# A gated linear-attention cell, a Fourier mixing layer and an MLP in one kernel: third weight piece joined after the fourth block's addition, one conversion fewer per piece, a decay load and some products moved

## The chip, the cores and the metric

The kernel runs on one core of one Trainium2 chip. The metric is the device time of one execution in microseconds (us); a comparison takes the median of several executions. The core's engines are TensorE (PE; PEld is its weight load), VectorE (DVE), ScalarE (ACT), GpSimd (POOL) and SyncE (SP), which here only issues DMAs. Each engine works through its own instructions in the order in which they were recorded.

## The reference

Inputs are four batches of 8 heads, 768 tokens and head size 40. A recurrent cell with exponential gates gives x of shape 4 x 768 x 320; then a Fourier mixing layer and an MLP with two weight matrices held as float64 (320 x 1280 and 1280 x 320) follow.

```
m_new = max(f_gate[t] + m, i_gate[t])
f_stab, i_stab = exp(f_gate[t] + m - m_new), exp(i_gate[t] - m_new)
C = f_stab * C + i_stab * outer(v[t], k[t]);  n = f_stab * n + i_stab * k[t]
y[t] = sigmoid(o_gate[t]) * (C @ q[t]) / max(|n . q[t]|, 1)
...
u   = x + real(fft(fft(x, axis=seq), axis=features))
un  = (u - mean(u)) / sqrt(var(u) + 1e-6)
out = u + relu(un @ w_ch1) @ w_ch2
```

## The kernel before

The recurrence is computed in chunks: 128 tokens (batch 0) or two half chunks of 64 (batches 1 to 3), with a state C carried from chunk to chunk. Per chunk, PE makes scores (ps), the products with the state (ph or hb) and the new state's part (pc); ACT makes the weights W by exponentials; GpSimd scales the queries with the decay (qg, L563, from the loaded Gb), scales the values (vw, L569), masks W (L578) and decays the state (L705); DVE adds to the state (L712), weighs (L717) and finishes x (L768 to L772, L759).

The mixing layer folds x (fe), multiplies with DFT tables along the sequence (pz, copied out as Z and Zt) and along the features (pu, L988). Six blocks of 128 tokens, in the order 0, 5, 1, 4, 2, 3, then go through: the addition of pu to x with mean and variance (`mix_add`, L990: L1004, L1011, L1012 in batch 0; L1006 to L1012 later), the centring on ACT (`mix_center`, uc, L1026), the turn by PE (`mix_turn`, L1037, into put or ph), and ACT's copy into uT (L1042). One row of blocks 1 and 4 needs products of its own: in batch 0 the fourth and fifth product of the second feature group go to hb and are copied by DVE (L1001, L1002) ahead of block 4's addition; in later batches ACT copies them (`mix_own`, L1017, L1018).

The MLP of batch 0 takes uT in ten groups (`IN_ORDER`, L1121): two features' blocks of three products each (L1135) and four quarter-array products for the remaining rows (`rest_products`, L1118). Then the outputs follow (L1273). Batch 0's MLP runs beside batch 1's recurrence. Batches 1 to 3 use sums of weights (L1201, L1330).

The weights come as 64-bit words in ten pieces of 128 x 640 (`class Piece`, L439), built into float32 on the chip: `take` splits exponent e (L463) and upper mantissa m (L465), `convert` turns both on ACT (L471, L473), `join` puts sign and exponent together (L480), adds the lower mantissa (L483) and multiplies (L487). Each piece is loaded by SP (L453, 640 KB) into one of two raw buffers, so a load waits for the L483 of the piece two before.

The order is written out by hand: `at(slot, phase, fn, ...)` enters a step in a plan, and `run` records all steps sorted by slot and phase. A slot is about one step of PE work; phases EVAC, FILL, MAIN and FILL_PE (0 to 3, with fractions between) order the steps within it. PSUM banks are taken in the order of a string (`turn`, L92) or by number. DMAs are issued by SP in the recorded order, on eight semaphores in turn: each issue also waits for the DMA eight before it.

The steps around the change, in the plan's words:

```
for part, (s, phase) in enumerate(((24, -0.1), (26, 0.3), (26, 0.32))):   # L1464
    at(s, FILL + phase, pieces[2].join, part)
at(s_feat[p] + 3, FILL_PE + 5.05, mix_feat, b, p, slice(3, 5))            # L1092: own rows, slot 26
at(a, FILL + 0.05 if b < 2 else MAIN + 0.55, mix_own, b)                  # L1101
at(t + 1 if c < 2 or b > 1 else s - 5, FILL, mlstm_load_decay, b, c)      # L825
```

Batch 0's additions stand in slots 24, 25, 26, 27, 28, 29 at FILL. So DVE records: take of piece 2, L480 of piece 2, additions one to three, L483 and L487 of piece 2, take of piece 3, addition four, additions five and six, join of piece 3.

Of the kernel before, what the change touches and what calls it, by code (L numbers as in the profile page):

```python
# [10 lines left out]
FP = mybir.dt.float32  # L11
# [3 lines left out]
AF = mybir.ActivationFunctionType  # L15
OP = mybir.AluOpType
# [5 lines left out]
NP = H // 2  # L22
# [35 lines left out]
def kernel(  # L58
# [15 lines left out]
    nc = tc.nc  # L74
# [26 lines left out]
    ebias = const.tile([L, 1], FP, name="ebias")  # L101
# [25 lines left out]
    def at(slot, phase, fn, *args):  # L127
        plan.setdefault((slot, phase), []).append((fn, args))
# [7 lines left out]
    EVAC, FILL, MAIN, FILL_PE = range(4)  # L136
# [302 lines left out]
    class Piece:  # L439
# [15 lines left out]
        def take(self):  # L455
            if self.float:
                return
            n = self.src.shape[1]
            words = self.raw.bitcast(U32).rearrange("p (m two) -> p m two", two=2)
            self.lo, self.hi = words[:, :, 0], words[:, :, 1]  # L460
            self.e = cp.tile([L, n], U32, name="e", tag="e", bufs=1)
            self.m = cp.tile([L, n], U32, name="m", tag="m", bufs=1)
            nc.vector.tensor_scalar(out=self.e, in0=self.hi, scalar1=20, scalar2=0x7FF, op0=OP.logical_shift_right,  # L463
                                    op1=OP.bitwise_and)
            nc.vector.tensor_scalar(out=self.m, in0=self.hi, scalar1=0xFFFFF, scalar2=None, op0=OP.bitwise_and)  # L465

        def convert(self, part=None):
            if self.float:
                return
            if part != 1:  # L470
                nc.scalar.activation(out=self.e, in_=self.e, func=AF.Relu, scale=2.0**23, bias=ebias)  # L471
            if part != 0:
                nc.scalar.activation(out=self.m.bitcast(FP), in_=self.m, func=AF.Copy, scale=2.0**-20, bias=1.0)  # L473

        def join(self, part=None):
            if self.float:
                return
            m = self.m.bitcast(FP)
            if part in (None, 0):
                nc.vector.scalar_tensor_tensor(out=self.e, in0=self.hi, scalar=0x80000000, in1=self.e,  # L480
                                               op0=OP.bitwise_and, op1=OP.bitwise_or)
            if part in (None, 1):
                nc.vector.scalar_tensor_tensor(out=m, in0=self.lo, scalar=2.0**-52, in1=m, op0=OP.mult, op1=OP.add)  # L483
            at_ = 0
            for d in self.dst if part in (None, 2) else ():
                r = slice(at_, at_ + d.shape[0])
                nc.vector.tensor_tensor(out=d, in0=m[r], in1=self.e.bitcast(FP)[r], op=OP.mult)  # L487
                at_ += d.shape[0]

    w1_pieces = [Piece([w1_sb[:, n]], w_ch1[:, n * 5 * L:(n + 1) * 5 * L]) for n in range(NFF // 2)]  # L490
# [326 lines left out]
    def plan_halves(b, s0, stride=3):  # L817
        at(s0 - 2, FILL + 0.7, halves_start, b)
        for c in range(NT):
            s = s0 + stride * c  # L820
            end = c == NT - 1
            t = 22 + 2 * c if b == 1 and c < 3 else s - 6
            at(t, FILL, mlstm_load, b, c)
            at(t, FILL, mlstm_load_max, b, c)
            at(t + 1 if c < 2 or b > 1 else s - 5, FILL, mlstm_load_decay, b, c)  # L825
            at(s - 2, FILL, mlstm_load_o, b, c)
            at(s - 2, FILL + 0.1, mlstm_scale_q, b, c)
            at(s - 2, FILL + 0.15, halves_alone, b, c)
            at(s - 1, FILL, mlstm_scale_v, b, c)
            early = (b, c) == (1, 0)  # L830
            at(*((27, FILL + 0.22) if early else (s - 1, FILL)), mlstm_exp, b, c, 0)
            at(*((28, FILL + 0.3) if early else (s - 1, FILL + 0.5)), mlstm_exp, b, c, NP)
            at(s, FILL, mlstm_mask, b, c)
            at(s, FILL_PE + 2.05, halves_scores, b, c)
            at(s, FILL_PE + 2.5, halves_to_state, b, c)
            for i in range(2):
                at(s + i, FILL + 0.05, halves_decay, b, c, i)
                at(s + 1 + i, FILL - 0.2, halves_add, b, c, i)
            at(s + 1, FILL, halves_weigh, b, c)
            if end:  # L840
                for fn, phase in ((halves_from_state, 0.22 if b == 1 else 0.1), (halves_between, 0.23 if b == 1 else 0.15),
                                  (halves_from_chunk, 0.3)):
                    at(s + (1 if b == 1 else 4), MAIN + phase, fn, b, c)
            else:
                at(s + 3, FILL_PE, halves_from_state, b, c)
                at(s + 3, FILL_PE + 0.5, halves_between, b, c)
                at(s + 3, FILL_PE + 3, halves_from_chunk, b, c)
            at(s + 3, FILL_PE + 0.6, mlstm_tanh, b, c)
            at(s + 4, FILL + 0.05 if b == 1 else MAIN + 0.4, mlstm_finish, b, c)
# [216 lines left out]
    def plan_mix(b, s0, x_done, s_feat, s_add, s_turn):  # L1066
        for j in range(TG):
            p = TG - 1 - j
# [18 lines left out]
        for p in range(TG):  # L1087
            for i in range(3) if b == 0 and p == TG - 1 else ():
                at(s_feat[p] + i, FILL_PE + 5.1, mix_feat, b, p, slice(i, i + 1))
            if b == 0 and p == TG - 2:  # L1090
                at(s_feat[p], FILL_PE + 4.06, mix_feat, b, p, slice(0, 3))
                at(s_feat[p] + 3, FILL_PE + 5.05, mix_feat, b, p, slice(3, 5))  # L1092
            elif b == 0 and p == 0:
                at(s_feat[p], FILL_PE + 4, mix_feat, b, p, slice(0, 2))
                at(s_feat[p], FILL_PE + 4.04, mix_feat, b, p, slice(2, 3))
            elif b > 0 or p < TG - 1:
                at(s_feat[p], FILL_PE + 4, mix_feat, b, p)
        for c, a, t in zip(ORDER, s_add, s_turn):
            at(a, FILL if b < 2 else MAIN + 0.5, mix_add, b, c)
            if b > 0 and c == TG - 2:  # L1100
                at(a, FILL + 0.05 if b < 2 else MAIN + 0.55, mix_own, b)  # L1101
            at(*(((32, EVAC + 0.1) if c == 3 else (a, FILL + 0.25) if c in (4, 2) else (t, FILL + 0.1)) if b == 0 else
                 (t, FILL + 0.1)), mix_center, b, c)
            at(t, FILL_PE + (5 if b == 0 or c in ORDER[:4] else -0.1), mix_turn, b, c)
            if b > 0:
                at(t, FILL_PE + 6, mix_turn_out, b, c)
            elif t < s_mlp:
                at(t + 1, FILL + 0.2, mix_turn_out, b, c)
            else:
                at(t + 1, EVAC, mix_turn_out, b, c)  # L1110
# [12 lines left out]
    def mlp_in(b, gr, f):  # L1123


        k = mixes[b]
        u = [uT_bufs[gr][:, ch].rearrange("p c t -> p (c t)") for ch in range(3)]

        n = IN_ORDER.index((gr, f // 2))
        ahead = n > 3 and n % 2 == 1  # L1130
        if f % 2 == 0:
            k.pm = k.pm_next if ahead else [bank("pm", [L, TG * L]) for _ in range(2)]
            k.pms[n] = k.pm
        for i, ch in ((1, 1),) if f % 2 else ((0, 0), (0, 1), (1, 0)):
            nc.tensor.matmul(k.pm[i], w1_block(ch, f // 2 * 2 + i), u[2 * ch], start=(ch == 0 and not ahead),  # L1135
                             stop=(ch == 1 and (ahead or n == 2)), skip_group_check=True)

    def mlp_in_rests(b, n, ahead):

# [225 lines left out]
    def plan_mlp(b, s):  # L1365
# [10 lines left out]
        for gr, n in IN_ORDER if b == 0 else ():  # L1376
            for f in (2 * n, 2 * n + 1):
                at(s, MAIN, mlp_in, b, gr, f)
                s += 1
            i = IN_ORDER.index((gr, n))  # L1380
            if i < 4 or i % 2 == 0:
                at(*((s, MAIN + 0.5) if i == 1 else (s - 1, MAIN + (-0.1 if i == 2 else 0.2))), mlp_in_rests, b, i, False)
                if i > 3:
                    at(s - 1, MAIN + 0.25, mlp_in_rests, b, i + 1, True)
            for f in (2 * n, 2 * n + 1):
                at(s + (i == 1), EVAC, mlp_relu, b, gr, f)
# [63 lines left out]
        at(66 if n == 3 else 57, FILL + 0.41, out_weight_sums, n)  # L1450

    when = [((2, 0.7), (4, 0.5), None), ((18.5, 0.7), (20, 0.7), (21, 0.6)), ((21.5, 0.7), (23, 0.15), None)]
    when += [((26, 0.7), None, (29, 0.5)), ((30, 0.7), (34, 0.7), (35, 0.6))]
    when += [((s, 0.7), (s + 1, 0.7), (s + 2, 0.6)) for s in (36, 39, 42, 48, 51)]
    pieces = w1_pieces + w2_pieces
    for n, (w, p) in enumerate(zip(when, pieces)):
# [4 lines left out]
                at(t[0], FILL + t[1], fn)  # L1461
    for part, s in enumerate((7, 10, 13)):
        at(s, FILL - 0.28, pieces[0].join, part)
    for part, (s, phase) in enumerate(((24, -0.1), (26, 0.3), (26, 0.32))):  # L1464
        at(s, FILL + phase, pieces[2].join, part)
    for part in range(2):
        at(27, FILL + (0.23, 0.3)[part], pieces[3].convert, part)

    early = [(3, mlstm_load, 3), (3, mlstm_load_o, 2), (4, mlstm_load, 4), (5, mlstm_load_decay, 3),
             (5, mlstm_load_decay, 4), (7, mlstm_load_o, 3), (7, mlstm_load, 5),  # L1470
# [159 lines left out]
```

## Time and profile before

| | us |
|---|---|
| median of 3 runs | 389.57 (388.89 to 389.93) |
| the profiled execution | 386.95 |
| its span, first to last instruction | 385.2 |
| PE busy, weight load | 373.1, 274.7 |
| DVE, ACT, POOL busy | 282.2, 176.7, 132.1 |
| granted TensorE clock | 0.999 |

The busy time and the load of the DMAs in four stretches (us from the span's start; the first holds the mixing of batch 0, the second batch 0's MLP beside batch 1's recurrence, the third the first outputs and the mixing of batch 1):

| stretch | length | PE | DVE | ACT | POOL | DMA share, GB/s |
|---|---|---|---|---|---|---|
| 45 to 63 | 18.0 | 14.11 | 16.36 | 11.52 | 3.55 | 0.92, 230 |
| 63 to 104 | 41.0 | 40.28 | 37.09 | 27.10 | 29.31 | 0.88, 245 |
| 104 to 146 | 42.0 | 40.34 | 34.14 | 13.43 | 17.36 | 0.45, 127 |
| 146 to 385.2 | 239.2 | 235.90 | 156.41 | 89.64 | 54.85 | 0.20, 59 |

A line of an engine in order of time reads: start, busy us, engine, line, operation, output<-input, shapes, count, and in brackets the idle time ahead of it and what ended that. Adjacent rows of one engine can overlap by some tenths.

### The profile page before, as it was taken

Reading aid. Unit: us, or ns where it says so; the run is one execution under the profiler, and the core shown is the slowest. Engines: PE = TensorE matmul, PEld = TensorE weight load, DVE = VectorE, ACT = ScalarE, POOL = GpSimd, SP = SyncE. Lnnn points to the kernel's source line nnn. Section 1 sums busy time; section 2 is a strip of 40 time slices with the busy share of each in tenths; the row PEclk is TensorE's granted clock in tenths of the full one; section 3 lists DMA queues with packets and bytes.
Section 4 is the critical chain, followed back from the end, with each engine's and each line's share of the span. In section 5 each row is a group of like instructions: output and inputs, shape, how many; then the busy total and the mean of one; then the engine's idle time right before and its main releaser. Section 6 shows DMA issues by size and latency. Waiting matters only on the chain.

```text
span 385.2 us, 11416 instructions
## 1 busy us (share of the span) xinstructions
PE 373.1 (97%) x4602; PEld 274.7 (71%) x4602; DVE 282.2 (73%) x662; ACT 176.7 (46%) x511; POOL 132.1 (34%) x238
## 2 busy tenths in 40 slices
PE   8999987999999989999999999999999999999996
PEld 6887554566567767756578999656588996546996
DVE  8798998799998584778873787877755785246652
ACT  5988766878262114574443144654530133545000
POOL 4665433875685124363421434561300000020000
PEclk9999999999999999999999999999999999999999
DMA  7869499699981333456001824440000011000000
GB/s 197 281 200 325 137 241 256 189 250 259 258 208 39 108 103 97 144 174 183 1 3 40 207 70 136 146 100 3 0 2 34 1 36 36 0 1 2 35 36 34
DMA packets 21761, 44.00 MB, mean 114 GB/s; under 512 B 3508, under 2 KB 9996, under 8 KB 21580
## 3 DMA queue, kind: packets, MB, share of 16 engines
q1 hardware_dynamic: 21708, 43.27, 39.3%
q8 instruction: 36, 0.59, 0.6%
q14 instruction: 17, 0.14, 0.1%
HBM read 39.16 MB, written 4.10 MB: 112 GB/s over the span
## 4 chain that ended last, share of the span: by engine, by line
PE 79%; DVE 13%; issue 1%; ACT 1%; POOL 0%; DVEq 0%; ACTq 0%; POOLq 0%
PE po L1330 22%; PE pm L1201 19%; PE pm L1118 7%; PE po L1273 7%; PE ph L582 5%; PE ps L582 4%; PE pm L1135 4%; PE pu L988 2%; PE pz L942 2%; PE put L1037 2%; DVE so L772 1%; PE hb L582 1%; PE pzt L942 1%; DVE stats L1011 1%; DVE x L759 1%
## 5 line engine op out<-in xcount | busy, mean ns | idle before, releaser
L1279 DVE SCALAR_TENSOR_TENSOR x<-po,rstd,x 128x160 f32<-128x160 f32 (+1 forms) x69 | 27.1, 393 | 38.4 <-PE po L1330 34.0
L1207 DVE TENSOR_TENSOR h<-h,pm 128x384 f32<-128x384 f32 x60 | 30.5, 549 | 24.7 <-PE pm L1118 11.4
L578 POOL TENSOR_SCALAR_AFFINE_SELECT W<-W 64x512 f32<-64x512 f32 x36 | 28.6, 796 | 38.8 <-ACT W L551 37.6
L1201 PE MATMUL pm<-uT,w_sb 128*128 128x384 f32 x90 | 37.5, 506 | 0.1
L551 ACT ACTIVATE W<-W,colT 128x64 f32<-128x64 f32 x144 | 36.6, 336 | 0.0
L705 POOL TENSOR_TENSOR C<-C,decB 128x164 f32<-128x164 f32 x33 | 18.3, 555 | 52.8 <-DVE C L712 48.6
L1273 PE MATMUL po<-w_sb,h 128*128 128x320 f32 x120 | 33.9, 433 | 0.0
L1118 PE MATMUL pm<-uT,w_sb 64*64 64x384 f32 x320 | 33.2, 497 | 0.0
L563 POOL TENSOR_TENSOR qg<-qk,Gb 128x512 f32<-128x512 f32 x21 | 27.0, 1285 | 12.1 <-DMA qk<-in_qkT 11.1
L1061 POOL TENSOR_TENSOR t<-rstd 128x6 f32<-128x6 f32 x12 | 3.5, 292 | 76.1 <-DVE v L1055 75.6
L1273 PEld LDWEIGHTS po<-w_sb,h 128*128 128x128 f32 x120 | 22.4, 190 | 9.1 <-issue 0.3
L1135 PE MATMUL pm<-uT,w_sb 128*128 128x384 f32 x80 | 28.5, 496 | 0.0
L1330 PE MATMUL po<-T,S 128*128 128x160 f32 x180 | 27.8, 301 | 0.2 <-DVE x L1279 0.2
L1330 PEld LDWEIGHTS po<-T,S 128*128 128x128 f32 x180 | 25.4, 190 | 1.3 <-DVE x L1279 0.4
L1330 PE MATMUL po<-w_sb,h 128*128 128x160 f32 x180 | 26.3, 300 | 0.0
L1330 PEld LDWEIGHTS po<-w_sb,h 128*128 128x128 f32 x180 | 25.2, 190 | 1.4 <-DVE x L1279 0.3
L1201 PEld LDWEIGHTS pm<-uT,w_sb 128*128 128x128 f32 x90 | 15.5, 189 | 12.8 <-DVE h L1207 5.3
L1256 ACT ACTIVATE h<-h 128x384 f32<-128x384 f32 x45 | 23.1, 519 | 2.9 <-DVE h L1207 2.9
L1118 PEld LDWEIGHTS pm<-uT,w_sb 64*64 64x64 f32 x320 | 11.0, 132 | 17.3 <-issue 14.3
L569 POOL TENSOR_TENSOR vw<-kvt,colT 128x328 f32<-128x328 f32 x23 | 19.5, 847 | 4.9 <-DVE shift L211 2.6
L1135 PEld LDWEIGHTS pm<-uT,w_sb 128*128 128x128 f32 x80 | 14.3, 190 | 9.6 <-issue 1.2
L582 PE MATMUL ps<-qk 40*64 40x64 f32 (+1 forms) x768 | 19.1, 235 | 0.0
(255 smaller groups left out, 826.1 us busy)
## 6 DMA issues: line engine op xcount, KB each, us to landing
kvt<-in_kv SPq DMA_DIRECT2D x24, 336.0 KB
qk<-in_qkT SPq DMA_DIRECT2D x48, 160.0 KB
raw<-in_w SPq DMA_DIRECT2D x10, 640.0 KB
Gb<-G_d SPq DMA_DIRECT2D x42, 128.0 KB
W<-M_d SPq DMA_DIRECT2D x36, 128.0 KB
so<-in_o SPq DMA_DIRECT2D x24, 160.0 KB
out<-x SPq DMA_DIRECT2D x23, 160.0 KB
ds_sb<-in_dft_s SPq DMA_DIRECT2D x1, 1158.0 KB
```

Of the source, the lines that this page charges most:

```text
L551: nc.scalar.activation(out=k.W[:, h, :], in_=M, func=AF.Exp, scale=-1.0, bias=colT[:, c, 0, b * H + h:b * H + h + 1])
L563: nc.gpsimd.tensor_tensor(out=k.qg[:, :, t], in0=k.qk[:, 0, :, t], in1=k.Gb[:, :, t], op=OP.mult)
L578: nc.gpsimd.affine_select(out=W, in_=W, compare_op=OP.is_ge, fill=0.0, base=base, pattern=[[0, H], [-1 if back else 1, LH]], channel_multi ...
L582: nc.tensor.matmul(out, w, x, start=start, stop=True, skip_group_check=True)
L1118: nc.tensor.matmul(banks[i][half(cols)], w1_rest(n)[half(i), half(cols)], u[half(i)], start=start, stop=not start, skip_group_check=True)
L1135: nc.tensor.matmul(k.pm[i], w1_block(ch, f // 2 * 2 + i), u[2 * ch], start=(ch == 0 and not ahead), stop=(ch == 1 and (ahead or n == 2)), ...
L1201: nc.tensor.matmul(bank, w, u, start=start, stop=True, skip_group_check=True)
L1207: nc.vector.tensor_tensor(out=h, in0=h, in1=bank, op=OP.add)
L1256: nc.scalar.activation(out=h, in_=h, func=AF.Relu, scale=-1.0)
L1273: nc.tensor.matmul(k.po[m], hidden(gr, f)[:, i * L:(i + 1) * L], w2_sb[:, f, :], start=(f == 0), stop=(f == NFF - 1))
L1279: nc.vector.scalar_tensor_tensor(out=u, in0=po, scalar=k.rstd[:, c:c + 1], in1=u, op0=OP.mult, op1=OP.add)
L1330: nc.tensor.matmul(po, a[:, f], w[:, f], start=start and f == 0, stop=f == half - 1, skip_group_check=True)
```

## The change

It does the following. (1) The third weight piece's join (pieces[2]) is recorded as a whole after the fourth block's addition (27, FILL + 0.13 to 0.15) and ahead of piece 3's take (27, FILL + 0.16); piece 3's conversion is one step. (2) The mantissa is no longer converted by ACT: `take` sets the bit above it as well, L483 adds the lower word scaled by 2^-32 to the integer, and the last multiplication brings a factor 2^-20, as a scalar_tensor_tensor in place of a tensor_tensor. (3) Batch 0's own-row products move ahead of the first turns (slot 24). (4) The decay load of batch 1's first chunk is issued in the slot of its other loads, ahead of a weight load. (5) In batch 1, block 0's centring is recorded ahead of the own-row copies; in batch 0 the centring of blocks 4 and 2 and the exponentials of batch 1's first chunk are re-ordered on ACT. (6) The quarter-array products of batch 0's groups 8 and 9 are no longer made ahead as a pair: group 8's come before its full products, group 9's in its own slot; batch 1's last chunk reads its state two slots later.

```
-            nc.vector.tensor_scalar(out=self.m, in0=self.hi, scalar1=0xFFFFF, scalar2=None, op0=OP.bitwise_and)
-        def convert(self, part=None):
+            nc.vector.tensor_scalar(out=self.m, in0=self.hi, scalar1=0xFFFFF, scalar2=0x100000, op0=OP.bitwise_and,
+                                    op1=OP.bitwise_or)
+        def convert(self):
             if self.float:
                 return
-            if part != 1:
-                nc.scalar.activation(out=self.e, in_=self.e, func=AF.Relu, scale=2.0**23, bias=ebias)
-            if part != 0:
-                nc.scalar.activation(out=self.m.bitcast(FP), in_=self.m, func=AF.Copy, scale=2.0**-20, bias=1.0)
+            nc.scalar.activation(out=self.e, in_=self.e, func=AF.Relu, scale=2.0**23, bias=ebias)
...
-                nc.vector.scalar_tensor_tensor(out=m, in0=self.lo, scalar=2.0**-52, in1=m, op0=OP.mult, op1=OP.add)
+                nc.vector.scalar_tensor_tensor(out=m, in0=self.lo, scalar=2.0**-32, in1=self.m, op0=OP.mult, op1=OP.add)
...
-                nc.vector.tensor_tensor(out=d, in0=m[r], in1=self.e.bitcast(FP)[r], op=OP.mult)
+                nc.vector.scalar_tensor_tensor(out=d, in0=m[r], scalar=2.0**-20, in1=self.e.bitcast(FP)[r], op0=OP.mult,
+                                               op1=OP.mult)
...
-            at(t + 1 if c < 2 or b > 1 else s - 5, FILL, mlstm_load_decay, b, c)
+            at(*((t, FILL + 0.02) if (b, c) == (1, 0) else (t + 1 if c < 2 or b > 1 else s - 5, FILL)), mlstm_load_decay, b, c)
...
-            at(*((27, FILL + 0.22) if early else (s - 1, FILL)), mlstm_exp, b, c, 0)
-            at(*((28, FILL + 0.3) if early else (s - 1, FILL + 0.5)), mlstm_exp, b, c, NP)
+            at(*((27, FILL + 0.227) if early else (s - 1, FILL)), mlstm_exp, b, c, 0)
+            at(*((32, EVAC + 0.15) if early else (s - 1, FILL + 0.5)), mlstm_exp, b, c, NP)
...
-                for fn, phase in ((halves_from_state, 0.22 if b == 1 else 0.1), (halves_between, 0.23 if b == 1 else 0.15),
-                                  (halves_from_chunk, 0.3)):
-                    at(s + (1 if b == 1 else 4), MAIN + phase, fn, b, c)
+                for fn, phase in (((halves_from_state, -0.3), (halves_between, -0.2), (halves_from_chunk, -0.05)) if b == 1 else
+                                  ((halves_from_state, 0.1), (halves_between, 0.15), (halves_from_chunk, 0.3))):
+                    at(s + (3 if b == 1 else 4), MAIN + phase, fn, b, c)
...
-                at(s_feat[p] + 3, FILL_PE + 5.05, mix_feat, b, p, slice(3, 5))
+                at(s_feat[p] + 1, FILL_PE + 4.95, mix_feat, b, p, slice(3, 5))
...
-                at(a, FILL + 0.05 if b < 2 else MAIN + 0.55, mix_own, b)
-            at(*(((32, EVAC + 0.1) if c == 3 else (a, FILL + 0.25) if c in (4, 2) else (t, FILL + 0.1)) if b == 0 else
+                at(a, FILL + 0.15 if b < 2 else MAIN + 0.55, mix_own, b)
+            at(*(((32, EVAC + 0.1) if c == 3 else (a, FILL + 0.225) if c in (4, 2) else (t, FILL + 0.1)) if b == 0 else
...
-        ahead = n > 3 and n % 2 == 1
+        ahead = n in (5, 7)
...
-                             stop=(ch == 1 and (ahead or n == 2)), skip_group_check=True)
+                             stop=(ch == 1 and (ahead or n in (2, 8, 9))), skip_group_check=True)
...
-            if i < 4 or i % 2 == 0:
-                at(*((s, MAIN + 0.5) if i == 1 else (s - 1, MAIN + (-0.1 if i == 2 else 0.2))), mlp_in_rests, b, i, False)
-                if i > 3:
+            if i < 4 or i % 2 == 0 or i == 9:
+                at(*((s, MAIN + 0.5) if i == 1 else (s - 1, MAIN + (-0.1 if i in (2, 8, 9) else 0.2))), mlp_in_rests, b, i,
+                   False)
+                if 3 < i < 8:
                     at(s - 1, MAIN + 0.25, mlp_in_rests, b, i + 1, True)
...
-    when += [((26, 0.7), None, (29, 0.5)), ((30, 0.7), (34, 0.7), (35, 0.6))]
+    when += [((27, 0.16), None, (29, 0.5)), ((30, 0.7), (34, 0.7), (35, 0.6))]
...
-    for part, (s, phase) in enumerate(((24, -0.1), (26, 0.3), (26, 0.32))):
+    for part, (s, phase) in enumerate(((27, 0.13), (27, 0.14), (27, 0.15))):
         at(s, FILL + phase, pieces[2].join, part)
-    for part in range(2):
-        at(27, FILL + (0.23, 0.3)[part], pieces[3].convert, part)
+    at(27, FILL + 0.23, pieces[3].convert)
```

## The prediction

> **What bounds the kernel now.** I read the page's busy shares, then PE's waits, then each engine in order of time around them. PE is busy 97% of the span, so time is won only in its waits or in what they are fed by. PE's longest waits:
>
> ```profile
> PE put L1037 <- ACT uc L1026: 2.8, 2, 1.5
> PE ph L1037 <- ACT uc L1026: 2.4, 1, 2.4
> PE ph L582 <- DVE x L759: 0.9, 1, 0.9
> ```
>
> Columns: us in total, times, longest. All three name turns (L1037) or the fourth chunk's reading of state. PE in order of time shows where:
>
> ```profile
> 53.24 0.55 PE L1037 MATMUL put<-ident,uc 128*128 128x128 f32 x3 [1.30 <-ACT uc L1026]
> ...
> 57.02 2.10 PE L1135 MATMUL pm<-uT,w_sb 128*128 128x384 f32 x6
> 61.57 0.55 PE L1037 MATMUL ph<-ident,uc 128*128 128x128 f32 x3 [2.45 <-ACT uc L1026]
> ...
> 104.14 0.68 PE L582 MATMUL ph<-C,qg 40*64 40x41 f32 x32 [0.86 <-DVE x L759]
> ...
> 144.94 0.55 PE L1037 MATMUL put<-ident,uc 128*128 128x128 f32 x3 [1.52 <-ACT uc L1026]
> ```
>
> The turn at 61.57 waits for the fourth block's addition. DVE's order shows what stands ahead of it:
>
> ```profile
> 50.57 0.83 DVE L480 SCALAR_TENSOR_TENSOR e<-raw,e 128x640 uint32<-128x640 uint32 x1 [0.49 <-ACT e L471]
> 51.31 0.48 DVE L1004 TENSOR_TENSOR x<-x,pu 128x320 f32<-128x320 f32 x1
> ...
> 54.70 1.90 DVE L483 SCALAR_TENSOR_TENSOR m<-raw,m 128x640 f32<-128x640 uint32 x1
> 56.64 0.97 DVE L487 TENSOR_TENSOR w_sb<-m,e 128x640 f32<-128x640 f32 x1
> 57.64 0.91 DVE L463 TENSOR_SCALAR e<-raw 128x640 uint32<-128x640 uint32 x1
> ...
> 59.57 0.49 DVE L1004 TENSOR_TENSOR x<-x,pu 128x320 f32<-128x320 f32 x1
> ...
> 66.47 0.63 DVE L463 TENSOR_SCALAR e<-raw 128x640 uint32<-128x640 uint32 x1 [0.79 <-DMA raw<-in_w]
> ...
> 70.41 1.20 DVE L480 SCALAR_TENSOR_TENSOR e<-raw,e 128x640 uint32<-128x640 uint32 x1 [1.77 <-ACT e L471]
> ```
>
> A third weight piece's join sits between additions three and four, and L483 takes 1.90 where others take 0.82: GpSimd's L563 starts at 54.64 beside it. After 70.41 DVE runs without a gap worth naming until 106; in 63 to 104 it is busy 37.1 of 41.0 us. At 144 the cause is ACT's order:
>
> ```profile
> 143.77 0.24 ACT L1017 COPY pu<-pu 1x161 f32<-1x161 f32 x1 [8.33 <-DVE x L1009]
> 144.04 0.28 ACT L1018 COPY pu<-ident 1x159 f32<-1x159 f32 x1
> 144.27 0.61 ACT L1026 ACTIVATE uc<-x 128x384 f32<-128x384 f32 x1
> ```
>
> The centring of block 0, whose addition ended at 138.2, stands behind two copies that need block 1's.
>
> **The change part by part.** *First additions.* The join's L480 leaves the place ahead of the first addition, which then waits only for its product (PE, 49.50 plus 0.8): 50.35 instead of 51.31. Three additions at 1.12 to 1.14 each, then two row copies (58.87 to 59.57: 0.70), then the fourth with its statistics (59.57 to 60.82: 1.25): ready at 55.7, not 60.8. The two products that feed the copies cost PE the same 0.56, now before the first turn instead of after the third, in its 1.30 wait. Turns one to three come about 1 us sooner; L1135 starts when the third is copied out: ACT's centring 53.85, turn 54.5, copy 55.1 plus 0.45, so 55.6 for 57.02. Its three products take 1.95, and the fourth turn, centred by 56.4, follows at 57.55 for 61.57: −4.0 at that place.
>
> *What is late next.* The join of piece 2 and the unpacking of piece 3 (0.71, 0.85, 0.86, 0.41, 0.41 from unhindered rows, 62.96 to 64.52 and 48.32 to 50.0: 3.24) now follow. The fifth addition starts at 58.9 and ends at 60.05. PE, after 2.0 of products and 0.9 of scores, is there at 60.45; its turn waits for centring and for ACT's copy of turn four behind it: 61.1. ACT then has centring six, four exponentials (0.95), a copy and the first relu (63.5), for which PE's third next product waits about 0.7. At the last turn PE is at 64.15 for 66.74: −2.6 left.
>
> *Decay load.* Two 128 KB loads go ahead of a 640 KB one on SP's queue; everything behind them keeps its place. Before, the weight load is issued at 48.31 and L563 starts at 54.64. Moving 0.64 MB behind at 230 GB/s (windows, 45 to 63) brings L563 2.8 sooner, to 51.8, and the weight piece later by 1.1: at about 54.7 (SP waits for it until 53.6 now) for a reader at 58.0. The three GpSimd products (3.6 there) then lie beside additions: L759, also fed from PSUM, keeps 0.49 beside L569 (at 76.24), and the statistics never exceed 499 ns in 24. Cost 0; without that cover the 1.08, 0.15 and 0.42 seen at 54.70 to 57.64 come back (1.65, on the fifth addition).
>
> *DVE's lead.* DVE reaches L463 of piece 4 at 63.9 for 65.7, but its load, issued at 59.91, lands at 66.4; the queue was full (DMA share 0.9), so I keep 66.3. Then L463, L465 and three state operations until 68.4. L480 needs ACT's conversion; before, ACT came to it at 69.56 after eight exponentials, now those start at 65.05 and end at 67.05. So L480 is at 68.4 for 70.41: −2.0. [...]
>
> *Down to 104.* DVE keeps its −2.0. PE needs DVE's x of the chunk before; at 99.24 it had 0.25 to spare, so PE's lead shrinks to 2.25. There the last chunk's state reading moves behind four products more (2.1 of L1135): x, due 102.1, is then there, and the 0.86 wait goes. At 108.7 PE leads by 3.1. The second half of the last two weight groups keeps its count and cost.
>
> *Own rows.* With the centring ahead of the two copies the 1.52 at 144.94 goes; the copies still start at 143.7, when their addition ends. From 146 PE is busy 235.9 of 239.2 and the rest moves with it.
>
> *Joins.* Ten L473 (0.72 each, 7.2 of ACT) vanish. ACT stands idle 1.6 after the first (at 20.2) and DVE paces the later ones, so 0 beyond what is counted. L465 gets a second operation like L463's: 0.49 both. L487 becomes the form of L483 and L480, 0.79 to 0.83 against 0.82: 0, bounds ±0.3 for ten.
>
> Sum: 2.25 + 0.86 + 1.52 = 4.6, less 0.1 for handovers: 4.5. Span 385.2 to 380.7; the profiled execution, 386.95, to 382.4. The median of the runs is 2.6 above that execution, so 389.57 − 4.5 = 385.1.
>
> **The rivals.**
> *The load eats it.* If the load lands as late as 66.47 and L480 again waits for ACT or the GpSimd until 70.4, DVE leads by nothing: 0.25 + 0.86 + 1.52 = 2.6, so 387.0. For: DVE waits there already. Against: the 1.77 is ACT's, and ACT is freed.
> *No cover.* The decay load is not sooner, or the three GpSimd products fall on the join: PE's lead at the last turn is 2.6 − 1.65 = 1.0; 1.0 + 0.86 + 1.52 = 3.4, so 386.2. It also stands for the change not doing what it says there.
> *More.* The load lands early and DVE follows PE: 4.0 + 0.86 + 1.52 = 6.4, so 383.2.
> *Slower.* DVE's lead shifts its long operations against GpSimd's in the five blocks of 73 to 104, where DVE has no slack. The dearest single collisions are 1.28 (L772, 1.77 at 28.75 against 0.49) and 1.08 (L483). One 1.28 more in each block is 6.4, time 391.5; from 0.9 per block on nothing is gained, from 1.15 it is slower by 1.2. Against: GpSimd's L705 is released by DVE's L712 in each block, so the pattern travels along, and four of five blocks already pay (L772 0.91). [...]
>
> **How the numbers follow.** Forecast (384 to 386.5) 0.55, the load eats it 0.13, no cover 0.12, more 0.10, slower 0.05, a part of the collisions that leaves it within 1.2 us, 0.05. What a measurement here can tell from no change is 0.3%, 1.2 us. Faster: 0.55 + 0.13 + 0.12 + 0.10 = 0.90; same 0.05; slower 0.05. The range takes in the rivals at 383.2, 386.2 and 387.0 with ±0.4 for the runs' own spread (388.89 to 389.93) and the joins: 382.8 to 387.6.
>
> **What would show it.** Right: no wait over 0.2 at PE's fourth turn, near 57.5; L483 of piece 2 at about 0.82; L563 before 52.5; a short wait (0.7) at the fifth turn; L480 of piece 4 near 68.4; no wait at the last chunk's state reading and at the first turn of the second batch. Wrong: L480 of piece 4 still at 70; L772 or L463 longer than 1.3 in 73 to 104; new PE waits over 1 us after 109, where I count none.

## The result, and the profile after

| | changed kernel | kernel before |
|---|---|---|
| median | 383.92 us (20 runs, 382.20 to 390.61) | 387.99 us (20 runs, 385.61 to 392.66) |
| ratio of the times | 0.9919, 95% interval 0.9893 to 0.9946 | |
| profiled execution, its span | 383.69, 381.9 us | 386.95, 385.2 us |

The ratio is worth 3.1 us (2.1 to 4.2), and the spans differ by 3.3. Predicted were 4.5 us; the predicted time, 385.1, was counted down from a median of three runs, 389.57, while the median over 20 is 387.99 (counted from that, it would have been 383.5). So the time lies in the range, and the gain is 1.4 us smaller than forecast.

PE's longest waits in the changed kernel, over the whole span (us in total, times, longest), are below; a wait at the kernel's start, 1.2 us, is the same before and after:

```profile
PE ps L581 <- POOL vw L568: 1.5, 1, 1.5
...
PE ph L1036 <- ACT uT L1041: 0.6, 1, 0.6
```

All waits of PE for the centring are gone, and one of 1.5 us has come that the forecast does not have. PE in order of time shows where (start, busy, engine, line; idle time ahead in brackets; the join's three lines are L478, L481 and L485 for L480, L483 and L487, and lines behind them are one less than before):

```profile
57.90 0.49 PE L1036 MATMUL ph<-ident,uc 128*128 128x128 f32 x3
...
61.33 0.55 PE L1036 MATMUL ph<-ident,uc 128*128 128x128 f32 x3 [0.57 <-ACT uT L1041]
...
63.79 0.91 PE L1134 MATMUL pm<-uT,w_sb 128*128 128x384 f32 x2 [0.62 <-ACT h L1152]
64.54 0.49 PE L1036 MATMUL ph<-ident,uc 128*128 128x128 f32 x3
...
71.05 0.52 PE L581 MATMUL ps<-vw,kvt 64*40 64x41 f32 x32 [1.51 <-POOL vw L568]
...
98.97 0.68 PE L581 MATMUL ph<-C,qg 40*64 40x41 f32 x32
...
104.75 0.68 PE L581 MATMUL ph<-C,qg 40*64 40x41 f32 x32
...
142.07 0.49 PE L1036 MATMUL put<-ident,uc 128*128 128x128 f32 x3
```

The last turn and the reading at 99 in the kernel before:

```profile
66.74 0.49 PE L1037 MATMUL ph<-ident,uc 128*128 128x128 f32 x3
...
99.24 0.68 PE L582 MATMUL ph<-C,qg 40*64 40x41 f32 x32
```

The fourth turn comes 3.7 us sooner (57.90 for 61.57), the last 2.2 (64.54 for 66.74). At 99 only 0.3 is left (98.97 for 99.24). The last chunk's reading (104.75) and the second batch's first turn (142.07) no longer wait. What waits at 71.05 is told by DVE:

```profile
56.46 0.82 DVE L481 SCALAR_TENSOR_TENSOR m<-raw,m 128x640 f32<-128x640 uint32 x1
...
66.08 0.49 DVE L463 TENSOR_SCALAR e<-raw 128x640 uint32<-128x640 uint32 x1 [2.45 <-DMA raw<-in_w]
66.49 0.49 DVE L465 TENSOR_SCALAR m<-raw 128x640 uint32<-128x640 uint32 x1
66.89 0.32 DVE L711 TENSOR_TENSOR C<-C,ps 128x164 f32<-128x164 f32 x1
...
68.22 1.45 DVE L478 SCALAR_TENSOR_TENSOR e<-raw,e 128x640 uint32<-128x640 uint32 x1
...
73.49 0.33 DVE L711 TENSOR_TENSOR C<-C,ps 128x164 f32<-128x164 f32 x1 [1.82 <-POOL x L754]
```

and by GpSimd:

```profile
67.29 0.47 POOL L704 TENSOR_TENSOR C<-C,decB 128x164 f32<-128x164 f32 x1 [1.86 <-DVE C L711]
67.71 1.27 POOL L562 TENSOR_TENSOR qg<-qk,Gb 128x512 f32<-128x512 f32 x1
68.93 0.79 POOL L676 COPY alone<-sp_sb 128x4 f32<-128x4 f32 x1
69.67 1.32 POOL L568 TENSOR_TENSOR vw<-kvt,colT 128x328 f32<-128x328 f32 x1
70.95 1.96 POOL L577 TENSOR_SCALAR_AFFINE_SELECT W<-W 64x512 f32<-64x512 f32 x2
73.00 0.46 POOL L704 TENSOR_TENSOR C<-C,decB 128x164 f32<-128x164 f32 x1
```

Read from right to left: PE waits for chunk 1's scaled values (L568). They stand on GpSimd behind a state product (L704), which waits 1.86 us for DVE's state addition (L711). That stands on DVE behind the unpacking of the fifth weight piece (L463), which waits 2.45 us for its load. The delay also comes back to DVE. From 67.29 GpSimd works without a pause worth naming for 6.2 us, up to the state product at 73.00 (L704), which ends at 73.46. DVE's next addition needs that product and starts at 73.49 after 1.82 us of waiting; the profile names L754, a small operation on GpSimd right behind it, and PE's product at 71.05 had ended at 71.57. DVE began the join at 68.22, 2.2 us sooner than before (70.41), and at 73.49 it is 0.28 sooner than before:

```profile
73.77 0.31 DVE L712 TENSOR_TENSOR C<-C,ps 128x164 f32<-128x164 f32 x1
```

### The profile page after: what moved, and what is told of

Same layout as the page of the kernel before. It is cut to its first block, busy times and chain, and to the rows that moved or that the text cites. A ratio compares the mean times of both kernels' runs of the same rounds, so it can differ in the third digit from the quotient of the medians.

```text
span 381.9 us, 11403 instructions
## 1 busy us (share of the span) xinstructions
PE 373.0 (98%) x4602; PEld 275.0 (72%) x4602; DVE 279.9 (73%) x662; ACT 170.8 (45%) x501; POOL 131.7 (34%) x238
## 4 chain that ended last, share of the span: by engine, by line
PE 84%; DVE 6%; POOL 2%; DMA 1%; issue 1%; ACT 1%; POOLq 0%; DVEq 0%
PE po L1329 22%; PE pm L1200 19%; PE po L1272 9%; PE pm L1117 7%; PE ph L581 5%; PE pm L1134 4%; PE ps L581 4%; PE pu L987 3%; PE pz L941 2%; PE hb L581 2%; PE put L1036 2%; PE pzt L941 1%; DMA raw<-in_w 1%; PE pz L953 1%; DVE stats L1010 1%
## 5 line engine op out<-in xcount | busy, mean ns | idle before, releaser
L577 POOL TENSOR_SCALAR_AFFINE_SELECT W<-W 64x512 f32<-64x512 f32 x36 | 28.1, 780 | 40.6 <-ACT W L550 31.6
L704 POOL TENSOR_TENSOR C<-C,decB 128x164 f32<-128x164 f32 x33 | 17.5, 530 | 51.0 <-DVE C L711 46.8
L1272 PE MATMUL po<-w_sb,h 128*128 128x320 f32 x120 | 33.9, 433 | 0.0
L1117 PE MATMUL pm<-uT,w_sb 64*64 64x384 f32 x320 | 32.7, 497 | 0.0
L562 POOL TENSOR_TENSOR qg<-qk,Gb 128x512 f32<-128x512 f32 x21 | 27.0, 1285 | 10.4 <-DMA Gb<-G_d 8.9
L1272 PEld LDWEIGHTS po<-w_sb,h 128*128 128x128 f32 x120 | 22.4, 190 | 9.1 <-issue 0.3
L1117 PEld LDWEIGHTS pm<-uT,w_sb 64*64 64x64 f32 x320 | 10.9, 132 | 16.3 <-issue 13.6
L568 POOL TENSOR_TENSOR vw<-kvt,colT 128x328 f32<-128x328 f32 x23 | 20.1, 875 | 4.4 <-issue 2.2
```

What stands on the lines that cost most here:

```text
L562: nc.gpsimd.tensor_tensor(out=k.qg[:, :, t], in0=k.qk[:, 0, :, t], in1=k.Gb[:, :, t], op=OP.mult)
L577: nc.gpsimd.affine_select(out=W, in_=W, compare_op=OP.is_ge, fill=0.0, base=base, pattern=[[0, H], [-1 if back else 1, LH]], channel_multi ...
L1117: nc.tensor.matmul(banks[i][half(cols)], w1_rest(n)[half(i), half(cols)], u[half(i)], start=start, stop=not start, skip_group_check=True)
L1272: nc.tensor.matmul(k.po[m], hidden(gr, f)[:, i * L:(i + 1) * L], w2_sb[:, f, :], start=(f == 0), stop=(f == NFF - 1))
```

## The experiments

Each kernel was run beside the kernel before on the same chip; the differences in us are the ratio's distance from one, times 388 us. To compare stages, one profile of each is cut at five places on PE: the first row product of the mixing (L988 before, L987 after; near 48 us), the sixth turn, the reading of state near 99, the first output product (L1273 or L1272), the second batch's first turn, and the end. PE's idle times that the profile puts down to nothing ("issue", see the last section) are taken out of the stage they stand in.

| kernel | to sixth turn | to 99 | to first output | to second batch's turn | to end |
|---|---|---|---|---|---|
| before | 19.00 | 32.50 | 9.30 | 36.40 | 240.26 |
| e1 own rows alone | 18.05 | 32.31 | 9.33 | 34.74 | 239.82 |
| e2 last chunk alone | 18.17 | 32.32 | 8.24 | 36.42 | 239.72 |
| e4 joins alone | 18.63 | 32.64 | 9.09 | 36.39 | 240.06 |
| e3 first batch, load, joins | 16.64 | 33.97 | 9.07 | 36.41 | 239.68 |
| g1 own rows and last chunk | 18.55 | 33.64 | 8.29 | 34.74 | 239.81 |
| changed | 16.66 | 34.43 | 8.37 | 34.73 | 239.83 |
| g4 changed, again | 16.65 | 33.80 | 8.24 | 34.70 | 240.27 |

**The parts alone, on the kernel before.** Own rows, in whole:

```
-                at(a, FILL + 0.05 if b < 2 else MAIN + 0.55, mix_own, b)
+                at(a, FILL + 0.15 if b < 2 else MAIN + 0.55, mix_own, b)
```

> The kernel before with one edit: the second batch's own-row copies behind the centring of its first block. The prediction's sum counts 1.52 us for it (the wait of PE's first turn at 144.94 goes, nothing behind takes its place): time -1.5 us, and no wait over 0.2 us at the first turn of the second batch. Rival: the products behind that turn wait for ACT's later copies, so that only a part (0.5 us or less) reaches the end; then a new PE wait of about 1 us stands between 146 and 160.

Measured: ratio 0.9964 (0.9935 to 0.9994), −1.4 us (−2.5 to −0.2). In the table it is 1.66 us, in the one stage that holds the wait, and the first turn of the second batch has no wait.

The last chunk's reading with the two weight groups (part 6 of the change):

```
...
-                    at(s + (1 if b == 1 else 4), MAIN + phase, fn, b, c)
+                    at(s + (3 if b == 1 else 4), MAIN + phase, fn, b, c)
...
-        ahead = n > 3 and n % 2 == 1
+        ahead = n in (5, 7)
...
```

> The kernel before with one edit: the last chunk's state reading later, and the second half of the last two weight groups not ahead. The sum counts 0.86 us (the wait at 104.14 goes): time -0.9 us. Rival: the chunk's heads come out later too, so that the second batch's first products start no sooner: time 0, and a new wait between 105 and 120.

Measured: 0.9976 (0.9943 to 1.0008), −0.9 us, an interval that alone leaves it open; in the table the stage from 99 to the first output is 8.24 for 9.30.

The first batch's order, the decay load and the joins without these two (the two diffs above undone in the changed kernel):

> The changed kernel with the own-row copies and the last chunk's reading as they were before: only the first batch's order, the sooner decay load and the joins remain. The prediction counts 2.25 us for these. The theory from the two traces: DVE and PE lead by 2.2 us at 65 to 68, but chunk 1's values product on GpSimd stands behind a state product that waits for DVE's state addition, which stands behind the unpacking of the fifth piece and so behind its load; PE waits 1.5 us there, DVE's lead falls to 0.3 us, and at 99 PE leads by 0.3 to 0.5 us. Then the time is -0.3 to -0.6 us against before. Rival: the lead survives on PE and only the later parts are smaller than counted: time -2 us or more.

Measured: 1.001 (0.9982 to 1.0038), 0.4 us slower, −0.7 to +1.5: 2 us of gain is ruled out. The stage to the sixth turn is 2.4 shorter than in the profile of before, and the next one gives 1.5 of it back. But in this kernel's profile it is not the chain of the theory that takes it: the fifth piece's load comes sooner (DVE's L463 at 64.29, after 0.66 us of waiting), and PE's product with chunk 1's values, at 69.37, does not wait. PE waits 0.36 us for DVE's state at 76.73, and the sixteen quarter-array products from 80.92 on take 2.52 us to the start of what follows, for 1.45 in the kernel before (82.48 to 83.93); the profile names 0.22 of that, as "issue". So the lead was lost by two ways, and one profile shows only one of them.

The joins' new form in the old places (the class's lines of the diff and the single conversion of piece 3):

> The kernel before with one edit: the joins' new form (the mantissa's unit bit on DVE, the scale in the last product, no second conversion on ACT), all in their old places. The prediction counts 0 with bounds of 0.3 us either way. Rival: ACT's freed 0.72 us at the fifth piece lets the join there start sooner (1.77 us of waiting for ACT before L480 at 70.41 falls to about 1.0), which leads DVE by up to 0.7 us and the end by up to 0.25 us; or the last product's new form is slower than the plain product (0.05 to 0.1 us each): +0.3 us.

Measured: 0.9984 (0.9949 to 1.0018), −0.6 us, no difference that can be told. ACT's freed time does not start the join sooner: its first operation comes at 70.49 behind 1.82 us of waiting for ACT (70.41, 1.77 before).

**The two later parts together, and the changed kernel again.** If the first batch is worth nothing, these two parts are the whole gain. The edit of the one is both diffs above on the kernel before; the other is the changed kernel as it is.

> The kernel before with the two later edits alone: the own-row copies behind the first centring, and the last chunk's state reading later. The prediction's terms for them are 1.52 and 0.86 us; its term for the first batch, the decay load and the joins, 2.25 us, is left out. Theory: that term is worth nothing by the end (the lead is lost at chunk 1, and behind it DVE's blocks set the pace), so that this kernel is within 0.6 us of the changed one on the same chip, -2.4 us or a little more against before. Rival, the prediction's sum: 2.25 us slower than the changed kernel.

> The changed kernel again, on the chip of the three others: its time beside theirs, -3 us against before as measured (interval 2.1 to 4.2). A second profile also shows what of the first varies from execution to execution: theory, the wait at chunk 1's values product follows the landing of the fifth piece's load (18.2 us behind the first row product in the first profile, with 1.51 us of waiting); landing by 17 us there would leave under 0.6 us of it.

Measured, on one chip: the two parts 384.15 us, 0.9912 (0.9884 to 0.9939); the changed kernel 383.66 us, 0.9908 (0.9877 to 0.9939). They differ by 0.5 us in the medians and 0.2 in the ratios; the rival's 2.25 is excluded. The second profile of the changed kernel shows the chain again: the load lands 0.7 us sooner, counted from the first row product (17.49 for 18.20), and the wait is 0.6 shorter:

```profile
70.38 0.52 PE L581 MATMUL ps<-vw,kvt 64*40 64x41 f32 x32 [0.88 <-POOL vw L568]
```

**Taking the new wait away.** First on DVE: the unpacking behind the state addition that GpSimd waits for.

```
-    when += [((27, 0.16), None, (29, 0.5)), ((30, 0.7), (34, 0.7), (35, 0.6))]
+    when += [((27, 0.16), None, (29, 0.5)), ((33, 0.08), (34, 0.7), (35, 0.6))]
```

> The changed kernel with one edit: on DVE the unpacking of the fifth piece (two operations that wait 2.45 us for its load) moved behind the first state addition and the scores' weighting of chunk 0 of the second stage. Theory: DVE's state addition then comes as soon as PE's product and GpSimd's decay are there (65.5 for 66.9), GpSimd's second decayed state at 65.9 for 67.3, the values product of chunk 1 ends near 69.0 for 71.0, ahead of the join: PE's wait of 1.51 us at 71.05 goes (at most 0.3 left), and 1.2 to 1.8 us of it are still there at 99 as far as DVE keeps them. Time against the changed kernel -0.8 to -1.8 us. Rival (the load alone limits): the join starts no sooner, DVE's later blocks stay where they were, so the time stays within 0.4 us of the changed kernel though the wait is gone.

Measured: 383.40 us, 0.9903 (0.9873 to 0.9932), against the changed kernel's 0.9919 and 0.9908: no difference beyond the intervals, as the rival said. But the rival's reason is not what the trace shows. The wait at chunk 1 is gone, PE reaches the products behind it 2.3 us ahead of before (70.81 for 73.11), and DVE finishes its fourth chunk 1.6 us sooner than before, counted from the first row product. The lead is lost one block later, in PE's order of time:

```profile
70.81 3.49 PE L1134 MATMUL pm<-uT,w_sb 128*128 128x384 f32 x10
74.23 0.88 PE L1117 MATMUL pm<-uT,w_sb 64*64 64x384 f32 x8
75.33 0.68 PE L581 MATMUL ph<-C,qg 40*64 40x41 f32 x32 [0.21 <-DVE x L758]
75.81 0.66 PE L581 MATMUL ph<-C,alone 40*64 40x41 f32 x16
76.83 0.69 PE L581 MATMUL ps<-qk 40*64 40x64 f32 x32 [0.36 <-DVE C L711]
...
81.02 2.03 PE L1117 MATMUL pm<-uT,w_sb 64*64 64x384 f32 x16
```

PE waits there for DVE's finished chunk (0.21) and for DVE's state (0.36), and the sixteen quarter-array products take 2.03 us for 1.52 before and in the changed kernel, with no wait that the profile names. From the next reading of state (85.11) to the one at 99, PE takes 13.2 us here, before, with the own rows alone and in the changed kernel, without a wait: what is left of the lead is settled by 85. DVE does not hold PE at 99 in these profiles: its fourth finished chunk (L758, 0.49 long) is done 0.2 to 0.8 us before PE reads. It is close behind, though: from the first finished chunk to the fourth DVE needs 22.2 to 22.3 us in all four, and the first comes 28.5 us behind the first row product before, 28.1 in the changed kernel, 27.0 here. PE's reading at 99 comes 0.6 sooner than in the changed kernel's profile, not 1.5.

Then on GpSimd: the values product into the idle time ahead of the mask; and both edits together.

```
-            at(s - 1, FILL, mlstm_scale_v, b, c)
+            at(*((32, FILL - 0.1) if (b, c) == (1, 1) else (s - 1, FILL)), mlstm_scale_v, b, c)
```

> The changed kernel with one edit: on GpSimd chunk 1's values product ahead of chunk 0's mask and decayed states, in GpSimd's idle 8 us. Theory: PE's 1.51 us wait for it goes, since nothing of DVE stands ahead of it any more; PE then waits at most 0.3 us. As DVE's unpacking still stands behind the load, the join starts at 68.2 as now and ends about 0.4 us sooner (one collision less); DVE's next state addition follows PE, 1.5 us sooner. Time against the changed kernel -0.8 to -1.8 us. Rival: the same as for the edit of the unpacking (within 0.4 us).

> Both edits together. If both take away the same wait, as the theory says, the time is that of the better of the two, within 0.3 us; if the load or the collisions have a price of their own, the two add (a further -0.5 us or more).

Measured: 384.83 us, 0.9928 (0.9896 to 0.9960), and 383.29 us, 0.9903 (0.9867 to 0.9939). The wait at chunk 1 goes in both, as the theory has it, and the time does not follow: neither differs from the changed kernel by what can be told, and the two edits do not add. The moved product has a price of its own: it falls beside an operation of DVE (in the first of the two L463 at 59.90 takes 0.91 us for 0.49, in the second L485 at 57.76 takes 1.24 for 0.82), and PE's fifth turn waits 0.98 us for 0.57 in both.

**The decay load back behind the weight load**, in the changed kernel:

```
-            at(*((t, FILL + 0.02) if (b, c) == (1, 0) else (t + 1 if c < 2 or b > 1 else s - 5, FILL)), mlstm_load_decay, b, c)
+            at(t + 1 if c < 2 or b > 1 else s - 5, FILL, mlstm_load_decay, b, c)
```

> The changed kernel with one edit: the decay load of the second stage's first chunk back behind the weight load, as before. The prediction priced the lost cover at 1.65 us on the fifth addition. The theory from the traces: GpSimd's three products fall on the join of the third piece (L481 of it near 1.9 us for 0.82), the fifth addition is up to 1.65 us later, but the fifth piece's load comes sooner than or as now and the lead is lost at chunk 1 anyway, so that the time is 0 to +0.5 us against the changed kernel. Rival, the prediction's: PE's lead at the last turn falls by 1.65 us and the end with it, +0.8 us or more.

Measured: 384.90 us, 0.9961 (0.9932 to 0.9990), 1.0 us above the changed kernel by the medians and 1.6 by the ratios. That is nearer to the prediction's rival (0.8 or more) than to the later theory (0 to 0.5), but the difference of the ratios has an interval of about 0.1 to 3.2 us, which excludes neither. GpSimd's products fall on the third piece's join, as DVE's order shows:

```profile
56.17 1.35 DVE L481 SCALAR_TENSOR_TENSOR m<-raw,m 128x640 f32<-128x640 uint32 x1
```

GpSimd's qg starts at 53.87 there (52.57 in the changed kernel), L481 takes 1.35 us for 0.82, and PE's fifth turn waits 1.15 for 0.57. The collision costs 0.5 us in place of the 1.65 that were priced, and in this profile PE's reading at 99 comes 0.8 us later (51.91 us behind the first row product for 51.09). The rest of the difference in time is not explained by one place.

**Load and conversion sooner.** The last two kernels should have started DVE's join earlier, and then made DVE's stretch shorter:

```
-            at(t, FILL, mlstm_load_max, b, c)
+            at(*((27, FILL + 0.75) if (b, c) == (1, 2) else (t, FILL)), mlstm_load_max, b, c)
-    when += [((27, 0.16), None, (29, 0.5)), ((30, 0.7), (34, 0.7), (35, 0.6))]
+    when += [((27, 0.16), None, (29, 0.5)), ((33, 0.08), (33, 0.9), (35, 0.6))]
```

The second has `(36, 39, 45, 48, 51)` for `(36, 39, 42, 48, 51)` besides.

> The changed kernel with the fifth piece's unpacking behind the first state addition and the scores' weighting, its load ahead of one load of the same queue (the mask's exponents of the third chunk), and ACT's conversion for it between the two groups of four exponentials. Theory (load and conversion hold DVE's join, and DVE's pace from that join on sets PE's place at 99): the join's first operation comes 0.6 to 1.2 us sooner than with the edit of the unpacking alone (20.9 us behind PE's first row product there), and PE's reading of state at 99 about 0.3 to 0.6 us sooner than in the changed kernel's profile (51.1 us behind that product). Time -0.3 to -1.0 us against the changed kernel. Rival (PE's own work sets the place at 99): no change there.

> The kernel with the sooner load, and the eighth piece's unpacking and join (some 3.4 us of DVE) one block later. Theory (DVE's pace in the blocks of 73 to 99 is what eats the lead): PE's reading of state at 99 comes 1 to 2 us sooner, at about 49 to 50 us behind the first row product, since PE alone needs 32.3 us from its sixth turn to there; the time follows only as far as the work moved does not return at the last chunk (0 to -0.5 us against the kernel with the sooner load), where PE then waits for DVE. Rival (PE is bound by its own work there): no change at 99.

Measured: 387.17 us, 1.0005 (0.9974 to 1.0037), and 389.02 us, 1.0028 (0.9991 to 1.0065): by the medians 3.5 and 5.4 us slower than the changed kernel on the same chip. The edit itself made the loss: the conversion now stands on ACT ahead of the copy of the last turn, which PE needs, and waits 3.8 us for DVE's unpacking. ACT in order of time, first kernel of the two:

```profile
68.11 0.83 ACT L471 ACTIVATE e<-e,ebias 128x640 uint32<-128x640 uint32 x1 [3.81 <-DVE e L463]
68.85 0.46 ACT L1041 COPY uT<-ph 128x384 f32<-128x384 f32 x1
```

PE waits 3.5 us for that copy in both. In the profile of the second the granted clock behind that wait is 0.52 (70 to 72 us, see the last section) and PE takes 4.32 us for the first's 2.83 to the next reading of state, a part of what it loses there beyond the first. So neither tells whether a sooner load or a lighter DVE would keep the lead; that stays open. The best time measured, with the unpacking moved or both edits (383.3 to 383.4), is not told apart from the changed kernel's.

## Why the prediction was right or wrong

**Own rows, 1.52: right.** 1.66 to 1.68 us in three pairs of profiles (36.40 to 34.73, 36.40 to 34.74, 36.42 to 34.74).

**The last chunk, 0.86: right.** The stage is 9.07 to 9.33 without the edit and 8.24 to 8.37 with it, about 0.9.

**Joins, 0 ± 0.3: not contradicted.** The run alone gives −0.6 with an interval of 2.7 us; the stages show no place for a gain.

**First additions and what is late next: right to half a microsecond.** First addition 50.50 (forecast 50.35), fourth turn 57.90 (57.55), fifth addition 58.98 (58.9), fifth turn 61.33 (61.1) behind the copy of turn four, the third product's wait 0.62 (0.7), last turn 64.54 (64.15).

**Decay load: the place right, the amount partly.** L562 starts at 52.57 (forecast 51.8, and "before 52.5"), L481 of the third piece takes 0.82 as forecast. Without the sooner load the same join loses 0.5 us on DVE, not 1.65, and the time 1.0 to 1.6 (0.1 to 3.2 by the interval).

**DVE's lead, −2.0 at the fifth piece's join: right.** It is at 68.22 (forecast 68.4), its load, issued at 59.13, landed at 66.08 (66.3), and ACT's conversion no longer holds it in that profile. In the two others of this order (e3 and g4) it starts at 68.22 and 68.17 and still waits for ACT, 1.19 and 0.81 us.

**"DVE keeps its −2.0" down to 104, so that PE leads by 2.25 at 99: this step failed.** PE's lead was 0.27 us there in the profile. Over all profiles of the old and the new order of the first batch (five and three of them, 51.2 and 50.7 us on the mean from the first row product to 99) it was about 0.5, with a scatter of 1.8 between executions of the old order. In the first profile DVE's lead fell from 2.2 us at the join to 0.28 at its next state addition.

The first thing that stood in its place is the chain through three engines at chunk 1. The forecast took the load as the limit of DVE and did not ask who waits behind DVE's waiting L463: it is GpSimd, and behind GpSimd both PE (1.51 and 0.88 us in the two profiles of the changed kernel) and DVE itself (1.82 in both). The second shows where the chain is not there, in e3 and with the unpacking moved: PE loses the lead between 75 and 85, in short waits for DVE (0.36 and 0.57 us in all) and in quarter-array products that take 1.07 and 0.5 us longer. Why they do is not shown; the old order has it too (g1, 1.89 us for 1.45). That part of the cause stays open.

Part of the 2.25 was not there to gain: the profile of before has the sixth turn 19.0 us behind the first row product, the four others of the same order 18.05 to 18.63. Its L483 of 1.90 us, with GpSimd's qg starting 0.06 us ahead of it, is 1.45, 1.08 and 0.94 in the three where qg starts 0.50, 0.88 and 1.01 us ahead, and 0.79 in the one where qg starts 1.29 us later.

Of the rivals, "the load eats it" has the arithmetic that came true, 2.6 us, but by another way: it has the join still at 70.4, and the join came at 68.22. The measured sum is 1.67 + 0.9 + 0.5 = 3.1, its last term from the profiles; by the times of the runs alone it is not told from nothing. The "slower" rival's collisions did not grow: L771 is 0.90 us on the mean of four blocks from 73 to 99, and its counterpart 0.91 before.

## What to carry to other kernels

When an engine's first instruction waits for a load, count what stands behind it on that engine and who waits for that: the load's price is paid by the last of them, here PE through DVE and GpSimd. A lead at one place is worth no more than what every engine behind it keeps: before carrying a lead across a stretch, look on each engine for a run without a pause, such as GpSimd's 6.2 us from 67.29 to 73.46, that begins behind the late instruction. When a wait is taken away, follow the engine to the next place where it meets another one. And a wait priced from one profile is one draw: look at whether its cause (a load's landing beside another engine's operation) varies from execution to execution.

## What the runs showed of the hardware that was not expected

PE stands still now and then for nothing that the profile shows, between two products of one group: 1.32 us at 105.78 with the own rows alone, 0.84, 0.63 and 0.73 at 83.00, 88.89 and 150.05 with both edits, 1.75 at 107.33 with the unpacking moved, 0.15 to 0.4 or none in the other profiles. They fall at different places in these profiles and sum to 2.2 us with both edits; whether they are behind the scatter of one kernel's times is not shown. The first sixteen quarter-array products of the block at 80 (L1117, L1118) look like the same: to the start of what follows they take 1.45 us in six of the fourteen profiles and 1.70 to 3.13 in the other eight, while the next sixteen, near 91, take 1.34 in all. Behind one of the pauses the granted clock is lower. The windows of the kernel with the unpacking moved (us, PE busy, PEld, DVE, ACT, POOL busy, granted clock, DMA share, GB/s):

```profile
106.00:108.00 2.00, 0.67 (x23) 0.62 (x24) 1.82 (x3) 0.00 (x0) 1.78 (x3) 1.00 0.81 192
108.00:110.00 2.00, 2.00 (x5) 1.18 (x5) 1.78 (x6) 0.49 (x1) 1.64 (x6) 0.58 0.67 202
110.00:112.00 2.00, 2.00 (x6) 1.33 (x5) 2.00 (x3) 0.78 (x2) 2.00 (x3) 0.57 0.72 198
112.00:114.00 2.00, 2.00 (x9) 1.39 (x8) 1.85 (x4) 1.96 (x9) 0.44 (x1) 1.00 0.90 252
```

The granted clock is 0.58 and 0.57 in the two windows from 108 to 112 us, behind the stall of 1.75 us, and that profile's next stage takes 36.2 us for 34.7. A wait of 2.45 us in the profile of before (61.57) and one of 1.51 in the changed kernel (71.05) have a clock of 1.00 behind them. The two kernels of the last experiment wait 3.5 us at the same place (69.36 and 68.88): in the profile of the first the clock stays at 1.00, in that of the second it falls:

```profile
70.00:72.00 2.00, 2.00 (x8) 0.62 (x10) 0.88 (x2) 0.74 (x4) 1.12 (x2) 0.52 0.03 9
```

From that wait to the next reading of state PE then needs 4.32 us (68.88 to 73.20), in the first 2.83 (69.36 to 72.19); the six products right behind it take 3.06 us for 2.20. Of the twelve runs of each of these two kernels, six and nine have a mean clock under 0.999; of the changed kernel's eight on that chip none has. So the length of a pause alone does not tell here whether the clock is lower behind it; what decides it is not shown.

DVE's unpacking beside GpSimd's qg took 1.60 us (L463 at 66.19, unpacking moved) for the 0.49 it takes with GpSimd idle (66.08, changed kernel), so moving an operation out of a wait can put it into a collision that costs 1.1.
